# A recurrence with a two-layer network behind it, on one core: the network's blocks go from 384 to 512 tokens, the middle layer is done in halves, and transposes of the later chunks move from TensorE to VectorE

## The chip, the core and the metric

The program runs on one core of a Trainium2 chip. The metric is device microseconds per execution. The kernel before was run three times: 488.08, 490.09 and 491.03 us, a median of 490.09. One more execution was recorded by the hardware profiler; all rows of the profile come from that one.

## The reference: what is computed

The inputs are r, k, v, w of shape batch 4 x heads 8 x sequence 768 x 48, u of heads 8 x 48, and the weights U (768 x 32), V (32 x 768), w1 (384 x 1536) and w2 (1536 x 384).

```
for t in range(S):                                    # a state of 48 x 48 per batch and head
    cur = einsum('bhd,bhe->bhde', u * k[t], v[t])
    y[t] = einsum('bhd,bhde->bhe', r[t], state + cur)
    state = w[t][..., None] * state + einsum('bhd,bhe->bhde', k[t], v[t])
x = y as (batch, 768, 384)                            # heads side by side
h = (x transposed @ U @ V) transposed                 # mixes the 768 tokens of a batch, rank 32
u2 = x + h
out = u2 + maximum(u2 @ w1, 0) @ w2
```

The sequence ahead is serial in the tokens; the mixing needs all tokens of a batch; the network (FFN) behind it needs each token for itself alone.

## The kernel before, in words

**Chunks.** The recurrence is cut into 24 chunks of 128 tokens, six for each batch (`chunk`). For each chunk VectorE runs two scans over the decay w (F, L367, and Q, L380) and scales r and k with them (rk, L387 and L392). TensorE then multiplies scaled k with scaled r to scores for each head (aps, L495), VectorE merges these into a tile A under a mask (L498), A's diagonal comes from r, k and u on other engines (dv, then L430 or L432), and two rounds of matmuls make the chunk's output y: A times v (L555 and L565), and the state of the chunks before times r (L578 and L582). The state is carried on in Z: k is transposed to have tokens on the partitions (four transposes of 128 x 128 in `turn_k`, trk, L482, copied to SBUF as kn by ScalarE), kn times v makes the chunk's addition (dS, L505), and VectorE adds and decays it (Z). The last chunk of a batch hands on no state, so its k isn't transposed. ScalarE copies y to xT (L598), which has channels on the partitions.

**Mixing.** xT of each chunk is transposed (`turn`, three transposes, trx, L616) and copied to xn (L620). For each batch `token_mix` multiplies xn of its six chunks with U (ga, L640), sums up four row groups (gb, L651), and splits the result into a high part and a remainder (gs). `make_u` multiplies it with V (hp, L690) and VectorE adds that to xT (L694).

**FFN.** It is done in 8 blocks of 384 tokens, two for each batch. All its factors are float32 numbers split into a high part and a remainder, and each product is made of three: high x high, remainder of the weight x high, high x remainder. `make_u` splits xT into u (L699 and L705). `ffn` makes 12 *up* steps for a block (f, L738), one for each 128 rows of the middle layer: nine matmuls of 128 x 128 weights against 384 tokens, into one of three PSUM tiles. For each, ScalarE or VectorE takes the maximum with zero as hh (L745 or L747) and VectorE the remainder hl (L751). Then, for each of three output tiles, four *down* steps of nine matmuls (L774) take in 3 of the 12 rows of the middle layer each, all four into the same PSUM tile, VectorE adds it to xT (`total`, L789), and SyncE sends the 128 x 384 piece out (`send`, L793). So there are 192 FFN steps, 1,728 matmuls, and 24 adds at L789. Twelve pairs of hh and hl are held at most.

**Weights.** They arrive as 64-bit numbers and are decoded on the chip, in 24 pieces for w1 and w2 and a few for U and V (`split_raw`): ScalarE, VectorE (L291 to L304) and GpSimd make a float32 number, ScalarE or VectorE the high part, GpSimd or VectorE the remainder (w1l and w2l, L321). This is work of the run's first part.

**Fillers.** `warm` (L180) issues bfloat16 matmuls that compute nothing that is used, into a PSUM tile that the next step overwrites. A step can have some of them ahead of it (`lead`).

**What sets the order.** Every piece of work is a step with its engine. A table of three-character entries, ORDER, gives the sequence in which all steps are issued; `plan` replays it. The first two characters are the step's number, the third says whether the step goes to its other engine and how many fillers stand ahead of it. Each engine executes its own steps in that sequence, and waits at a step until what it needs is there. `plan` also counts the buffers of each kind against `caps` (3 PSUM tiles for the FFN, `ffn`; 12 pairs of the middle layer, `hid`; 1 PSUM tile for transposes, `tr`; and so on).

Of the kernel before, what the change touches and what calls it, by code (L numbers as in the profile page):

```python
# [33 lines left out]
RAW_BUFS, TURNING, CVA_BUFS, KR_BUFS, W_BUFS, RK_BUFS = 7, 4, 3, 2, 2, 4  # L34
# [3 lines left out]
def channel_order():  # L38
# [25 lines left out]
    "06m09R02K09q03206n02509016r0AG01s03312o02L01t08R06p06u06s02O01u09116t01v06q06x02708T02M13D01w08U06v02606y06w"
    "09E02q08V02802Q02903F02R02A06z02B09N02S02f02C01x12D12p06++8r03E02r07108s13G06-"
    "02s02h03H07002T08t07407212U01O03I02V17507303J02g02i03K03402t07602j08u01Q07702k09g08v08W13603L18g07802l01P079"
    "08e09p08h02u03e0A702m03M02v01R08k82n18f02w13507A01S08l03709S11T03808w13f08m03907B03g03h08n09H08i03O03i09J09T"
    "09208j19G03A09409301U03V07C03B09503C01V01W09903N03P07D09M13W03X03Q09I09K07M09A03R0A607N07Q09L19B0AZ09607E07O"
    "09C07R09i03S09W09707S07F09D07T17G0AF09X07P17U09809b07V03Y07W09c09j09U09d03Z09k1D409V09l07X17Y09m09e07Z09Y03a"
    "0AY09f07b07a09n1A809Z03b07e07c09a0Ah03c17d03d17f09o13T19wCA909y09x03j09+0AB03U07g08609-"  # L70
    "03k0AA03l07H0AE1A019r1Ab0AM07h09s1AN0Ag1Ac19t03m0AQ07i1Ai07I09u07j0AH1AC07k08S0AD0D30Ad0AI07J07l07m09v0AJ07n"
    "09z0DD0AK0DC0Aj1AL1AO0Ae07o0A10AP0DT0Af1A20Aa07p0DE0Ao0DU0AR07K0AS1DF07q07L0Dc0Ak1D608707r0Al0DG0Am1Dd07s07t"
    "0E30DW0A30A40DB17u07w0A50DX0D707v0An0D80Db0Ap0Av07x0De0AT07y0D90AU0D50880AV0Dw0E41Dv0DY0DA1AW07z0Df0AX0DH0Dg"
    "0Aq0E51EV07+1DI0E20Ar07-"
    "0DV0Dy0DJ0Dh1EM0800E60As0Dz0E11Ex0DK0DL0EW1810DZ0At0Eo0DN0820Di0Au0EL0D+0DM0830Da1DO1EX1D-"
# [12 lines left out]
    "0IY0Fk0Fo0Iy0Jg1K50Fl0K00JK0Fp0IZ0Jk0JL0Iz0Jh0Fh0JN0J-0Fi0Jl0Fj0JO0K61Jw0I+0Fm1K80JM0I-"
    "0Fn1Fq0K70Jm0Gk0Fr0Fs0K90Go1Gl1Fv0Gs1Gp1Gt1Jn0Fy0Fw0Ft1Jo1Fx0Fu0F-"
    "0Fz1F+0GQ0G01G10G20G50G31G40G80G60G70GR0G91GA0GB0GE0GC0GD0GH0GF0GG0GK0GI0GJ0GN0GL0GM0GS0GO0GP0GT0GW0GU0GV0GX"  # L90
    "0GY0GZ0Gc0Ga0Gb0Gd0Ge0Gf0Gu0Gg0Gh0Gx0Gv1Gw0G+0Gy0JP0Gz0H10G-"
    "0H00JQ0H21H40JR0H30H70H50H60HA0H80H90HS0HB1HC0HT0Jp0Jq0HD0Jr0HG0HE1HF0HJ0HH0HI0HM0HK0HL0HP0HN0HO0HU0HQ1HR0Js"
    "0KA0Jt0KB0KF0KC0HV0KD0HW0HY0KE0HX0KG0HZ0KH0KI0Ha0KJ0KK0KL0KP0Hb0KM0KQ0KN1KR1KT0KO0He0Hc0KU0Hd0KS1KV0LN0KW1LR"
    "0Hf0LO0LS0LP0LT0LQ0Hg0LU1Hh0LV0KX0Hi0LW0Hj0LX1LY1Ka0KY0KZ0Kd0Kb1Kc0Kg0Ke0Kf0L50Kh0Ki0Kj0Km0Kk1Kl0Kp0Kn1Ko0L6"
    "0Kq0Kr0Ks0Kv0Kt1Ku0Ky0Kw0Kx0L70Kz0K+0K-"
    "0L20L00L10L30L40L80LB0L90LA0LC0LD0LE0LH0LF0LG0LI0LJ0LZ0LK0La1Lb0Lc0LL0LM0Lf0Ld0Le0Li0Lg0Lh0M70Lj0Lk0Ll0Lo0Lm"
    "1Ln0Lr0Lp1Lq0M80Ls0Lt0Lu0Lx0Lv1Lw0L+0Ly1Lz0M90L-"
    "0M00M10M40M21M30M51M60MA0MD0MB0MC0ME0MF0MG0MJ0MH0MI0MK0ML0MM0MN0MO0"
# [52 lines left out]
def rwkv_moe_kernel(ctx, tc, wT, rkT, vN, rkN, uB, uT, uD, U, V, w1, w2, out):  # L151
# [9 lines left out]
    hidp = pool("hidp", 24)  # L161
# [20 lines left out]
    def lead(to):  # L182
        if leading[0]:
# [4 lines left out]
    make_identity(nc, ident)  # L188
    maskf = const.tile([P, P], F32, name="maskf")
# [26 lines left out]
    caps = dict(w=W_BUFS, rk=RK_BUFS, kr=KR_BUFS, v=2, F=2, Q=1, A=2, dv=2, kn=2, Z=2, tr=1, aps=1, y=1, dS=1, ffn=3, xT=3, xn=NCH,  # L216
                hid=12, raw=RAW_BUFS, turning=TURNING, cva=CVA_BUFS, g4=1, gs=1, qd=1)

    def step(name, eng, fn, after=(), take=(), use=(), alt=None):

        s = Step(name, eng, fn, after, list(take), list(use), alt)
        steps.append(s)
        return s
# [105 lines left out]
    def chunk(g):  # L329
# [657 lines left out]
```

## Time and profile before

| | us |
|---|---|
| three runs | 488.08, 490.09, 491.03 |
| the profiled execution | 493.23 |
| its span (first to last instruction) | 491.4 |
| TensorE matmuls busy | 467.2 (95%) |
| TensorE weight loads busy | 419.8 (85%) |
| VectorE busy | 315.2 (64%) |
| ScalarE busy | 169.5 (34%) |
| GpSimd busy | 114.6 (23%) |

PE is TensorE's matmuls, PEld its weight loads, which run beside them, DVE is VectorE, ACT ScalarE, POOL GpSimd, SP SyncE; a small q behind one of these names is its queue of issued work. A matmul's recorded duration reaches from its start to its modelled end, and matmuls overlap in the pipeline: the 576 matmuls of the first FFN group are recorded at 344 ns each but take up 158.1 us together. So the time from one matmul to the next is read from starts or from long unbroken stretches, not from a matmul's duration. A group's row gives the line of the program, the engine, the operation, the tile written and the tiles read, the shapes and the number of instructions, then after the bar the busy time in us and the mean duration in ns, and after the second bar the idle time of that engine just ahead of these instructions, with what ended most of it. The chain of waits is the work that ended last, followed back from the last instruction.

### The profile page before, as it was taken

The page shows a single profiled execution, that of the slowest core. Times are in us where ns is not written, and L with a number is a line of the kernel's source. Part 1 is how long each engine was busy: PE and PEld are TensorE (multiplying, and loading weights), DVE is VectorE, ACT ScalarE, POOL GpSimd, SP SyncE. Part 2 cuts the span into 40 slices and gives each one's busy share as a digit, 9 for nine tenths or more (in the row PEclk, how much of TensorE's full clock was granted, in tenths as well). Part 3 has the DMA queues.
Part 4 walks back from the last instruction along what each step waited for, and adds up shares of the span by engine and source line. Part 5 has one row for each costly group of instructions (what it writes and reads, how often), then busy time and mean ns, then how long its engine had stood idle before and what let it go on. Part 6 is the DMA issues. An engine that isn't in the chain of part 4 may idle for free.

```text
span 491.4 us, 9913 instructions
## 1 busy us (share of the span) xinstructions
PE 467.2 (95%) x4116; PEld 419.8 (85%) x4116; DVE 315.2 (64%) x543; ACT 169.5 (34%) x430; POOL 114.6 (23%) x106
## 2 busy tenths in 40 slices
PE   7799889998999999999999999999999999999994
PEld 3577647887889889999988989799999989999994
DVE  8966888999899989961486983683123344412420
ACT  5666665755543453310146430531011221101000
POOL 3513444424454435400061400130000010000000
PEclk9656999999999999999999999999999999999998
DMA  8825864544423583400254630300000000000001
GB/s 295 258 70 173 232 234 128 176 130 147 148 85 88 168 269 111 108 1 16 79 166 120 192 99 33 99 21 0 17 32 1 1 34 17 1 27 23 0 18 37
DMA packets 20644, 47.38 MB, mean 96 GB/s; under 512 B 2480, under 2 KB 8880, under 8 KB 20592
## 3 DMA queue, kind: packets, MB, share of 16 engines
q1 hardware_dynamic: 20592, 46.67, 30.0%
q8 instruction: 34, 0.56, 0.5%
q14 instruction: 18, 0.15, 0.1%
HBM read 41.94 MB, written 4.72 MB: 95 GB/s over the span
## 4 chain that ended last, share of the span: by engine, by line
PE 57%; DVE 21%; DMA 10%; ACT 4%; issue 4%; POOL 2%; SPq 0%; POOLq 0%; DVEq 0%; ACTq 0%
PE f L774 23%; PE f L738 22%; DMA raw_w<-in_w 4%; DMA w<-in_wT 3%; DVE Q L380 3%; DVE F L367 3%; DMA rk<-in_rkT 3%; PE aps L495 2%; DVE cva_w L297 2%; DVE hl L751 2%; PE y L555 1%; PE trk L482 1%; PE y L565 1%; DVE rk L392 1%; PE dS L505 1%
## 5 line engine op out<-in xcount | busy, mean ns | idle before, releaser
L738 PE MATMUL f<-u,w1h 128*128 128x384 f32 x576 | 158.1, 344 | 2.0 <-DVE hl L751 1.4
L738 PEld LDWEIGHTS f<-u,w1h 128*128 128x128 f32 x576 | 105.4, 188 | 4.8 <-DVE hl L751 2.5
L774 PE MATMUL f<-hh,w2h 128*128 128x384 f32 x288 | 100.0, 347 | 0.0
L738 PE MATMUL f<-u,w1l 128*128 128x384 f32 x288 | 97.6, 339 | 0.0
L774 PE MATMUL f<-hh,w2l 128*128 128x384 f32 x288 | 97.5, 339 | 0.0
L751 DVE SCALAR_TENSOR_TENSOR hl<-f,hh 128x384 fp32r<-128x384 f32 x96 | 52.5, 552 | 34.6 <-ACT hh L745 33.4
L745 ACT ACTIVATE hh<-f 128x384 fp32r<-128x384 f32 x56 | 27.3, 488 | 128.0 <-PE f L738 128.0
L774 PE MATMUL f<-hl,w2h 128*128 128x384 f32 x288 | 66.3, 338 | 0.0
L774 PEld LDWEIGHTS f<-hh,w2h 128*128 128x128 f32 x288 | 54.0, 188 | 3.5 <-issue 1.7
L774 PEld LDWEIGHTS f<-hh,w2l 128*128 128x128 f32 x288 | 54.1, 188 | 0.3
L738 PEld LDWEIGHTS f<-u,w1l 128*128 128x128 f32 x288 | 54.1, 188 | 0.2 <-DVE w1l L321 0.2
L774 PEld LDWEIGHTS f<-hl,w2h 128*128 128x128 f32 x288 | 52.0, 188 | 0.0
L789 DVE TENSOR_TENSOR xT<-f,xT 128x384 f32<-128x384 f32 x24 | 13.3, 553 | 55.6 <-PE f L774 55.5
L747 DVE TENSOR_SCALAR hh<-f 128x384 fp32r<-128x384 f32 x40 | 22.2, 554 | 32.2 <-PE f L738 32.0
L304 POOL TENSOR_TENSOR cva_w<-cva_w,raw_w 128x384 int32<-128x384 int32 x24 | 29.8, 1247 | 40.8 <-DVE cva_w L297 21.7
L432 POOL TENSOR_SCALAR_AFFINE_SELECT A<-dv 128x512 f32<-128x512 f32 x23 | 19.5, 855 | 84.4 <-PE y L565 46.4
L498 DVE COPY_PREDICATED A<-maskf,aps 128x1024 f32<-128x1024 uint32 x24 | 31.4, 1307 | 7.1 <-PE aps L495 4.6
L367 DVE TENSOR_TENSOR_SCAN F<-w,resets 128x517 f32<-128x517 f32 x24 | 32.5, 1354 | 2.5 <-DMA w<-in_wT 1.4
L430 ACT ACTIVATE A<-ident,dv 128x128 f32<-128x128 f32 x100 | 31.6, 390 | 5.1 <-DVE dv L461 2.3
L495 PE MATMUL aps<-rk 48*128 48x128 f32 x384 | 30.6, 303 | 2.2 <-DVE rk L392 1.3
L495 PEld LDWEIGHTS aps<-rk 48*128 48x128 f32 x384 | 25.7, 204 | 6.1 <-issue 2.6
L380 DVE TENSOR_TENSOR_SCAN Q<-w,qd 128x516 f32<-128x516 f32 x24 | 30.5, 1273 | 0.0
(117 smaller groups left out, 596.3 us busy)
## 6 DMA issues: line engine op xcount, KB each, us to landing
rk<-in_rkT SPq DMA_DIRECT2D x24, 512.0 KB, 4.6
raw_w<-in_w SPq DMA_DIRECT2D x24, 384.0 KB, 4.2
kr<-in_rkN SPq DMA_DIRECT2D x18, 384.0 KB, 3.7
w<-in_wT SPq DMA_DIRECT2D x24, 258.5 KB, 2.9
v<-in_vN SPq DMA_DIRECT2D x24, 224.0 KB, 3.2
out_dram<-xT SPq DMA_DIRECT2D x24, 192.0 KB, 1.9
raw_V<-in_V SPq DMA_DIRECT2D x6, 96.0 KB, 5.7
raw_U<-in_U SPq DMA_DIRECT2D x1, 192.0 KB, 5.0
```

The source lines that it names most:

```text
L304: lambda: nc.gpsimd.tensor_tensor(out=d["to"].bitcast(I32), in0=d["a"].bitcast(I32), in1=d["e"], op=ALU.add),
L367: nc.vector.tensor_tensor_scan(out=F[:, ::-1], data0=st["w"][:, ::-1], data1=resets[:, ::-1], initial=1.0, op0=ALU.mult, op1=ALU.add)
L380: nc.vector.tensor_tensor_scan(out=st["Q"], data0=st["w"][:, 0:n], data1=qd, initial=0.0, op0=ALU.mult, op1=ALU.add)
L430: nc.scalar.activation(A[:, i, j], ident, AF.Copy, scale=dv[:, NP * i + j : NP * i + j + 1])
L432: nc.gpsimd.affine_select(out=A[:, i], in_=dv[:, NP * i : NP * i + NP].unsqueeze(2).broadcast_to([P, NP, P]), pattern=[[0, NP], [1, P]], c ...
L495: nc.tensor.matmul(aps[:, i, j, :], rk[r, 1, j, :], rk[r, 0, j, :], start=True, stop=True)
L498: nc.vector.copy_predicated(flat(st["A"]), mask8, flat(st["aps"]))
L738: nc.tensor.matmul(ps, wt[:, f, ct, :], u[ct][:, z], start=(n == 0), stop=(n == 8))
L745: nc.scalar.activation(hh, d["ps", f], AF.Relu)
L747: nc.vector.tensor_scalar(out=hh, in0=d["ps", f], scalar1=0.0, scalar2=None, op0=ALU.max)
L751: nc.vector.scalar_tensor_tensor(out=hl, in0=d["ps", f], scalar=0.0, in1=hh.bitcast(F32), op0=ALU.max, op1=ALU.subtract)
L774: nc.tensor.matmul(d["o", ct], wt[:, 4 * ct + part, f - 3 * part, :], hid[f][z], start=(part == 0 and n == 0), stop=(part == 3 and n == 8),)
```

## The change

**Wider blocks.** The 24 chunks are put into 6 FFN blocks of 4 chunks, 512 tokens, over the batches' borders: blocks 1 and 4 hold two chunks each of two batches. Their mixing product and add come in two parts of 256 tokens (`pieces_of`, `make_u`), and their output goes out in two transfers. All tiles of the FFN become 512 wide. The mixing still goes by batch.

**Half the middle layer at a time.** A block does six up steps, then for each output tile two down steps and an add to xT, then the other six up steps, two down steps and another add. Eight pairs of hh and hl are held at most (12 before). The buffers for raw weights, which u uses as well, become 6 (7), each wider; those for xn become 4 (6). There are now 144 FFN steps, 1,296 matmuls of 512 columns, and 36 adds of 512 columns (L871).

**Transposes.** The k of chunks 12 to 23 (ten of them carry a state) and the x of chunks 18 to 23 are transposed by VectorE, straight from SBUF to SBUF: four steps for each chunk, each of four instructions that turn 32 x 32 pieces (`turn_blocks`, L661). These are 160 instructions for k, of 32 partitions x 128 elements, and 96 for x, of 32 x 96. The transposes on TensorE and ScalarE's copies of them go for these chunks.

**Not used.** A way of making a weight's remainder on TensorE is in the code for the pieces in SPLIT_PE, which is empty. One more constant tile (`minus`) is made by one ScalarE instruction.

**A new ORDER.** The table is written anew. It issues 197 fillers instead of 154. Three places of it follow.

TensorE at the start of the first block, as the change has it (f_0_0 and f_0_1 are the PSUM tiles of the first and second up step, trk those of a transposed k; L185 are the fillers):

```order
L185 MATMUL f_0_0_1061<-resets 128x384
L819 MATMUL f_0_0_1061<-u_0_995,w1h 128x512
...
L819 MATMUL f_0_0_1061<-u_2_1056,w1h 128x512
L185 MATMUL trk_1096<-resets 128x384
...
L509 MATMUL trk_1096<-ident,rk_828 128x128 x4
L537 MATMUL dS<-v_998,kn_1116 48x48 x8
...
L185 MATMUL f_0_1_1293<-resets 128x384
L819 MATMUL f_0_1_1293<-u_0_995,w1h 128x512
...
L819 MATMUL f_0_1_1293<-u_2_1056,w1h 128x512
L819 MATMUL f_0_2_1321<-u_0_995,w1h 128x512
```

Between the first and the second up step of the block stand the recurrence of several chunks and fillers; from the second on the up steps follow one another. Before, sixteen FFN steps stood ahead of the scores of chunk 6.

TensorE before, where the k of chunk 14 (rk_2144) is transposed between two up steps:

```order
L738 MATMUL f_1_0_1_2516<-u_0_1_2437,w1h 128x384
L738 MATMUL f_1_0_1_2516<-u_0_2_2453,w1h 128x384
L482 MATMUL trk_2532<-ident,rk_2144 128x128 x4
L738 MATMUL f_1_0_2_2537<-u_0_0_2374,w1h 128x384
L738 MATMUL f_1_0_2_2537<-u_0_0_2374,w1l 128x384
```

and in the change, where that part of the run has only the scores of chunk 13 (rk_1882) between FFN steps:

```order
L819 MATMUL f_1_6_2363<-u_1_2199,w1h 128x512
L819 MATMUL f_1_6_2363<-u_2_2225,w1h 128x512
L527 MATMUL aps_2385<-rk_1882 128x128 x8
L855 MATMUL f_1_0_0_2328<-hh_3_2321,w2h 128x512
L855 MATMUL f_1_0_0_2328<-hh_3_2321,w2l 128x512
```

The transposes of k have left TensorE's row of work here; the FFN steps before and after are wider.

VectorE in the change, where the k of chunks 12 and 13 (rk_1801 and rk_1882) is transposed:

```order
L530 COPY_PREDICATED A_1841<-maskf,aps_1873 128x1024
L661 STREAM_TRANSPOSE kn_1922<-rk_1801 32x4x32 x4
L443 TENSOR_TENSOR kr_1834<-kr_1834,u_rep 128x384
L577 TENSOR_TENSOR Z_1885<-Z_1885,tots 128x384
L440 TENSOR_TENSOR kr_1704<-kr_1704 128x384
L394 SCALAR_TENSOR_TENSOR F_1946<-w_1341,resets 128x517
L661 STREAM_TRANSPOSE kn_1922<-rk_1801 32x4x32 x4
L871 TENSOR_TENSOR xT_392<-f_0_0_2_1629,xT_392 128x512
L443 TENSOR_TENSOR kr_1704<-kr_1704,u_rep 128x384
L430 RECIPROCAL qd<-F_1946 128x4
L661 STREAM_TRANSPOSE kn_2015<-rk_1882 32x4x32 x4
```

The four steps of a chunk's transpose stand apart, with scans, merges and the FFN's adds (L871) between them.

The diff, cut to its core:

```
-RAW_BUFS, TURNING, CVA_BUFS, KR_BUFS, W_BUFS, RK_BUFS = 7, 4, 3, 2, 2, 4
+RAW_BUFS, TURNING, CVA_BUFS, KR_BUFS, W_BUFS, RK_BUFS, XN_BUFS, HID = 6, 4, 3, 2, 2, 4, 4, 8
+BLOCKS = (4, 4, 4, 4, 4, 4)
+TW = 4 * P
+TURN_K_DVE, TURN_X_DVE = range(12, 24), range(18, 24)
 ORDER = (
-    "3n03p01g01F04C00001X03s03r04E03y03u03o03v04D01h01i04e01j01G01k01H05301I01l04L04d04F00200103t13q01Z01J04H01m0"
+    "0003r00G00Y01p03n03q04C03p00100203o00300H00404E00500I00J00604D00a00K00Z00L00701q00b00M01r03y03s02N04L00c01s0"
...
-    hidp = pool("hidp", 24)
+    hidp = pool("hidp", 2 * HID)
...
+        def turn_k_blocks(i):
+            if i == 0:
+                st["kn"] = sb2.tile([P, NP, P], F32, tag="kn", name=f"kn_{g}")
+            turn_blocks(st["kn"], st["rk"][:, 1], i)
...
-            btr = Buf("tr")
-            kt = step("KT " + nm, "PE", turn_k, [ks], take=[btr, buf["kn"]], use=[buf["rk"]])
-            kn = step("KN " + nm, "ACT", copy_k, [kt], use=[buf["kn"], btr])
+            if g in TURN_K_DVE:
+                kn = ks
+                for i in range(4):
+                    kn = step(
+                        "KD " + nm, "DVE", lambda i=i: turn_k_blocks(i), [kn], take=[buf["kn"]] if i == 0 else [],
+                        use=[buf["rk"], buf["kn"]],
+                    )
+            else:
+                btr = Buf("tr")
+                kt = step("KT " + nm, "PE", turn_k, [ks], take=[btr, buf["kn"]], use=[buf["rk"]])
+                kn = step("KN " + nm, "ACT", copy_k, [kt], use=[buf["kn"], btr])
...
+    def turn_blocks(to, src, i):
+        for j in range(4):
+            nc.vector.transpose(
+                to[32 * j : 32 * j + 32, :, 32 * i : 32 * i + 32], src[32 * i : 32 * i + 32, :, 32 * j : 32 * j + 32]
+            )
...
-        for ct in range(NCT):
-            bps = Buf("ffn")
-            for part in range(4):
+        for half in range(2):
+            for f in range(6 * half, 6 * half + 6):
...
+            for ct in range(NCT):
+                bps = Buf("ffn")
+                for part in (2 * half, 2 * half + 1):
...
+                o = sums[ct] = step(
+                    f"O {q}.{half}.{ct}", "DVE", total, [prev, sums.get(ct)] + d["uls"], use=[bps, bx], width=W
                 )
...
+                if half:
+                    step(f"OUT {q}.{ct}", "SP", send, [o], use=[bx], width=W).n = len(d["parts"])
```

More of the change, by code (lines that the diff above doesn't have):

```diff
@@ L99 @@
+    "0Ks1Kt0Kl0Kk0Km0Ko0Kn0Kp0Ku0Kq0Kx0Kv1Kw0K+0Ky1Kz0L10K-"
+    "0L00L40L21L30L70L50L60L80LB0L90LA0LC0LF0LD0LE0LG0LH0LI0"
 )
@@ L602, in chunk, with pieces_of @@
+        bx = xbuf[q]
+        x = step("XE " + nm, "ACT", out_x, [y] + (xs_done[g - 1, "x"] if pos else []), take=[bx] if pos == 0 else [], use=[buf["y"], bx])
+        xs_done[g, "x"] = [x]
         xs_done[b, c] = [x]
-        turn(b, c, [x], bx, buf["xn"])
+        turn(b, c, [x], q, pos, bx, buf["xn"])
+    place_of = [(q, i) for q, n in enumerate(BLOCKS) for i in range(n)]
     blocks, xbuf, xs_done, xns = {}, {}, {}, {}
-    def turn(b, c, after, bx, bxn):
-        blk, cc = divmod(c, TB // P)
-        btr = Buf("tr")
-        d = {}
+    def pieces_of(q):
+        gs = [g for g, (r, _) in enumerate(place_of) if r == q]
+        for b in sorted({g // NCH for g in gs}):
+            mine = [g for g in gs if g // NCH == b]
+            lo = (mine[0] - gs[0]) * P
+            yield b, slice(lo, lo + len(mine) * P), (mine[0] % NCH) * P
@@ new lines, in turn_blocks, with turn, blocks_of_x @@
+    def turn_blocks(to, src, i):
+        for j in range(4):
+            nc.vector.transpose(
+                to[32 * j : 32 * j + 32, :, 32 * i : 32 * i + 32], src[32 * i : 32 * i + 32, :, 32 * j : 32 * j + 32]
+            )
+    def turn(b, c, after, q, cc, bx, bxn):
+        btr = Buf("tr")
+        d = dict(buf=bxn)
+        xns[b, c] = d
+        def blocks_of_x(i):
+            if i == 0:
+                d["xn"] = sb2.tile([P, NCT, P], F32, tag="xn", name=f"xn_{b}_{c}", bufs=XN_BUFS)
+            turn_blocks(d["xn"], blocks[q][:, :, cc * P : (cc + 1) * P], i)
+        if b != "g" and b * NCH + c in TURN_X_DVE:
+            last = after
+            for i in range(4):
+                last = [step(
+                    f"XD {b}.{c}", "DVE", lambda i=i: blocks_of_x(i), last, take=[bxn] if i == 0 else [], use=[bx, bxn],
+                )]
+            d["steps"] = last
+            return
@@ L705, in low @@
                 ENG[eng].tensor_tensor(
-                    out=u[:, 1], in0=blocks[b, blk][:, ct, :], in1=u[:, 0].bitcast(F32), op=ALU.subtract
+                    out=u[:, 1], in0=blocks[q][:, ct, 0:W], in1=u[:, 0].bitcast(F32), op=ALU.subtract
                 )
-            nm = f"{b}.{blk}.{ct}"
-            hp = step(
-                "HP " + nm, "PE", mix, [gs["step"], hp] + ready.get(("V", blk), []), take=[bhp], use=[gs["buf"]],
-            )
-            xs = [s for c in range(3 * blk, 3 * blk + 3) for s in xns[b, c]["steps"] + xs_done.get((b, c), [])]
@@ L714, in make_u @@
-            ad = step("UADD " + nm, "DVE", add, [hp] + xs, use=[bhp, bx])
-            uh = step(
-                "UH " + nm, "ACT", high, [ad] + ups[-1:], take=[bu], use=[bx], alt="DVE"
-            )
+            nm = f"{q}.{ct}"
+            uh = step("UH " + nm, "ACT", high, ads[ct] + ups[-1:], take=[bu], use=[bx], alt="DVE", width=W)
             ups.append(uh)
-            ul = step("UL " + nm, "Pool", low, [uh], use=[bx, bu], alt="DVE")
+            ul = step("UL " + nm, "Pool", low, [uh], use=[bx, bu], alt="DVE", width=W)
@@ L880, in general @@
             for blk in range(2):
-                make_u("g", blk)
-                ffn("g", blk, dst=dst)
+                make_u(("g", blk), [("g", slice(0, TB), blk * TB)])
+                ffn(("g", blk), dst=dst)
+            first = next(s for s in steps if s.name == "GA g.0")
+            steps.remove(first)
+            steps.insert(next(n for n, s in enumerate(steps) if s.name == "XT g.4"), first)
             for s in steps:
@@ L897, in rwkv_moe_kernel @@
         token_mix(b)
-        for blk in range(2):
-            make_u(b, blk)
-            ffn(b, blk)
+        for q in range(len(BLOCKS)):
+            last = max(g for g, (r, _) in enumerate(place_of) if r == q)
+            if last // NCH == b:
+                make_u(q, list(pieces_of(q)))
+                ffn(q)
     with tc.manual_schedule():
```

328 lines of the change are left out of this document (177 added, 151 removed).

## The prediction

> **What bounds the kernel now.** I read the busy times by stage first, then the chain that ended last, then single matmuls on the timeline, then the groups by shape. The stages:
>
> ```profile
> 0.00:72.00 72.00, 59.79 (x659) 42.63 (x660) 57.65 (x94) 46.82 (x128) 28.14 (x30) 0.81 0.66 215
> 72.00:113.00 41.00, 39.01 (x222) 32.36 (x220) 38.95 (x81) 24.25 (x56) 15.39 (x15) 1.00 0.43 136
> 113.00:202.00 89.00, 86.47 (x920) 76.45 (x921) 83.55 (x136) 39.57 (x102) 42.51 (x37) 1.00 0.46 141
> 202.00:324.00 122.00, 120.76 (x1313) 110.72 (x1314) 79.69 (x131) 39.24 (x103) 26.24 (x24) 1.00 0.30 92
> 324.00:485.00 161.00, 161.00 (x1007) 157.63 (x1005) 54.77 (x103) 19.64 (x42) 2.32 (x3) 1.00 0.04 15
> ```
>
> The columns are length, then busy time of matmuls, weight loads, VectorE, ScalarE and GpSimd, then the granted clock. From 113 us on TensorE is busy 86.47 of 89, 120.76 of 122 and 161 of 161 us at clock 1.00: it sets the end. VectorE is second, 38.95 of 41 and 83.55 of 89 us, then ever less. Between 72 and 113 us the first FFN block waits for weights that VectorE splits, and filler matmuls stand in the gaps. The chain agrees, and gives the price of an FFN matmul:
>
> ```profile
> 205.31 0.44 PE trk L482 x4
> ...
> 208.93 0.33 PE trx L616 x3
> 209.25 12.72 PE f L738 x72
> 221.97 11.13 PE f L774 x63
> 233.10 0.49 PE dS L505 x16
> 233.59 1.09 PE aps L495 x16
> ...
> 235.18 0.59 PE trk L482 x4
> ```
>
> Each row is a start, a length and what TensorE did. 12.72 / 72 and 11.13 / 63 are both 0.1767 us from one matmul of 384 columns to the next. What a block of 512 costs depends on why that is not less. The fillers, bf16 with as many columns, go faster, and the edge between an FFN matmul and a transpose tells more:
>
> ```profile
> 71.02 1.62 PE L180 MATMUL f<-resets 128*128 128x384 bf16 x9 [0.30 <-DVE xT L694]
> L180 PE MATMUL f<-resets 128*128 128x384 bf16 x83 | 14.2, 326 | 0.3 <-DVE xT L694 0.3
> ...
> 204.62 0.69 PE L738 MATMUL f<-u,w1h 128*128 128x384 f32 x3
> 204.97 0.53 PEld L482 LDWEIGHTS trk<-ident,rk 128*128 128x128 f32 x4
> 205.15 0.60 PE L482 MATMUL trk<-ident,rk 128*128 128x128 f32 x4
> 205.47 0.19 PEld L738 LDWEIGHTS f<-u,w1h 128*128 128x128 f32 x1
> 205.59 0.19 PEld L738 LDWEIGHTS f<-u,w1l 128*128 128x128 f32 x1
> ...
> L616 PEld LDWEIGHTS trx<-ident,xT 128*128 128x128 f32 x72 | 8.9, 147 | 4.8 <-ACT xT L598 3.2 <-ACT junk L396 0.2 <-ACT raw_w L278 0.2
> ```
>
> Nine fillers take 1.62 us; less the last one's 0.326, eight periods of 0.162 us. The FFN's matmuls are 15 ns slower. It could be their weight load, shown as 0.19 us and back to back. But the third FFN matmul starts at about 204.97, the transpose's load is issued with it, such a load takes 0.15 us, and still the transpose starts only at 205.15, 0.18 later. And behind the short transposes the next FFN load follows its forerunner after 0.12 us (205.47, 205.59), not 0.177. So the 384-column FFN matmul itself holds the array for about 0.177 us, and the load hides behind it.
>
> **The change, part by part.** *Width.* 1,728 matmuls of 384 columns become 1,296 of 512. The trace has no FFN matmul of another width, so the price has two ends. If the 15 ns come per column, 0.1767 x 512/384 = 0.2356 us. If they come per matmul, 128 more columns at the fillers' 0.162/384 add 0.054: 0.2304. No quoted row decides; I take the middle, 0.233. Per token that is only 1% less than now.
>
> The Trainium skill, "TensorE: Matmul & The Clock Gate", section "Back-to-back issue gap", gives N/2.4 + 2.5 ns for a warm matmul, 162.5 at 384 columns and 215.8 at 512. The fillers' 162 agrees with it, the FFN's 177 does not. By it the 1,287 matmuls counted below would take 277.7 us.
>
> *Front.* The new order starts one up step, waits, and from the second up step on carries no fillers but the 18 ahead of the second block. What must be done by then is VectorE's, so I price its steps by their groups' mean durations: 103.7 us of them stand ahead of the scores of chunk 6 in the order before, which began at 113.52, and 101.1 us ahead of the second up step now. At one busy microsecond per microsecond, as in 72 to 113 us, that step starts at 111.
>
> ```profile
> 113.52 0.49 PE L495 MATMUL aps<-rk 48*128 48x128 f32 x4 [1.28 <-DVE rk L392]
> 484.51 0.69 PE L774 MATMUL f<-hl,w2h 128*128 128x384 f32 x3
> 485.83 0.33 SPq L793 DMA_DIRECT2D out_dram<-xT  x1
> ```
>
> *TensorE from there.* Before, 113.52 to 484.51 + 0.69 = 485.2 is 371.7 us. All FFN steps but 16 lie in it: 1,584 x 0.1767 = 279.9. The other 91.8 are the recurrence, the mixing and waits. Now 143 FFN steps of 9 are left: 1,287 x 0.233 = 299.9, so 20.0 more, because only one step instead of 16 is done by then. The other work shrinks, since more chunks are done and transposes have left TensorE: 15 groups of four transposes of k less (0.44 and 0.59 in the chain; 0.45 taken: 6.8), 7 of x (0.33 there; 0.30 taken: 2.1), 2 score groups (1.09: 2.2), 3 state updates (0.49: 1.5), one inner product (its twelve matmuls estimated at 0.9), 3 mixing products more (estimated 0.5): 13.0. That leaves 78.8, with waits as they are. The moves alone give 10 x 0.45 + 6 x 0.30 = 6.3 of it.
>
> *VectorE.* The moved transposes become 160 of 32 x 128 elements and 96 of 32 x 96. The trace has none; the nearest copies:
>
> ```profile
> L205 DVE COPY sel<-sel 128x96 f32<-128x96 f32 x1 | 0.3, 252 | 0.0
> L461 DVE COPY dv<-trd 128x8 f32<-128x8 f32 x2 | 0.3, 159 | 0.8 <-PE trd L454 0.8
> L694 DVE TENSOR_TENSOR xT<-hp,xT 128x384 f32<-128x384 f32 x24 | 12.5, 546 | 1.3 <-PE hp L690 1.3
> L751 DVE SCALAR_TENSOR_TENSOR hl<-f,hh 128x384 fp32r<-128x384 f32 x96 | 52.5, 552 | 34.6 <-ACT hh L745 33.4
> L789 DVE TENSOR_TENSOR xT<-f,xT 128x384 f32<-128x384 f32 x24 | 13.3, 553 | 55.6 <-PE f L774 55.5
> ...
> sum 485.00, PE 467.02 PEld 419.80 DVE 314.61 ACT 169.53 POOL 114.60; mean PE 467.02 PEld 419.80 DVE 314.61 ACT 169.53 POOL 114.60
> ...
> span 491.4 us, 9913 instructions
> ```
>
> 93 ns for 88 elements make 0.252 at 96 and 0.286 at 128 alone. In a row each starts before the last ends: 24 adds of L694 are 12.5 us busy, not 13.1, and three in a row save 0.07 apiece. I take 0.18 and 0.21, together 51 us; the ends are the elements alone (0.10 and 0.14: 32) and no overlap (70). The second add of each output makes 36 wide ones of about 0.69 (0.553 and 128 elements more) out of 24: 11.5 more. The remainders L751 lose 3. So VectorE's 314.6 busy us become about 374. It comes where TensorE covers it: by the order 217 us of mean durations, 206 busy (314.6 busy are 330.8 by means), stand between the second up step and the scores of the last chunk, where TensorE has 222. That is 93%, as in 113 to 202 us, so I charge nothing. Without that cover each microsecond over 222 goes to the end. In VectorE's queue the remainders and adds that free the FFN's three PSUM buffers stand behind the transposes, and TensorE's next step behind those.
>
> *Nothing on the path.* ScalarE loses 16 copies and was at 39.57 of 89. GpSimd's wider subtractions fit 42.51 of 89. The output moves the same bytes. The 43 more fillers (7 us) stand in waits for VectorE, counted in the 111. Fewer buffers for the middle layer (8 for 12) go with only six halves held at once. The last add is 0.1 wider, and 0.1 goes to its transfer.
>
> *Sum.* 111 + 299.9 + 78.8 + (491.4 - 485.2) + 0.2 = 496.1 against a span of 491.4: 4.7 more. The profiled execution took 493.23, the runs' median is 490.09, so 494.8 for the median: 495.
>
> **Rivals.** *The load was the bound after all (B).* For it: loads are 157.63 of 161 busy, and 0.19 is longer than 0.177. The Trainium skill, "Perfetto Trace Analysis", section "Identifying the Most-Contended Engine", would judge TensorE by that share. Against it: the starts at 205.15 and 205.59. Then 512 columns stream at the fillers' rate, 0.162 x 4/3 = 0.216: 1,287 x 0.017 = 21.9 less. TensorE then has only 210 in the stretch where VectorE has 206, and I give 5 back to waits: 478.
>
> *The order pays (C).* The other 91.8 us hold about 13 of waits, since its steps priced singly make 79. If the new order takes two thirds of these, and VectorE's idle 14 us before 72 us are halved so that the second up step starts at 104, 16 less: 479. For it: a table written for several courses of events. Against: the front has as much VectorE work ahead as before, and the middle of the run more.
>
> *VectorE becomes the bound (D), slower.* Place: chunk 12 on, where each transpose of k stands in four pieces between scans and adds. If they overlap nothing (70 us), VectorE has about 223 of TensorE's 222 there, and the state update waits for the last piece. TensorE then loses what it does where VectorE has 94%, 2.5 of 89, and as much again for the late state updates, 12 in all over 222: 507. It decides from about 0.28 us a transpose on.
>
> **How the numbers follow.** A measurement here tells about 1% (5 us) from no change. My case (A) has 0.48: 495, own range 487 to 502, half of it within 1%, nearly the rest slower. B has 0.20, 0.18 of it faster and 0.02 within. C has 0.12, 0.10 faster and 0.02 within. D has 0.20, 0.18 slower and 0.02 within. Of A's 0.48, 0.02 is faster, 0.24 within, 0.22 slower. So faster by over 1%: 0.02 + 0.18 + 0.10 = 0.30; within: 0.24 + 0.02 + 0.02 + 0.02 = 0.30; slower: 0.22 + 0.18 = 0.40. B and C reach down to 472, D up to 511; the range is 471 to 510.
>
> **What would show it.** In the profile after: the 512-column matmuls about 0.233 apart (0.216 speaks for B); the second up step of the first block at about 111 us (104 for C); transposes at 0.2 to 0.29 us each and VectorE at or under 93% of the stretch up to the last chunk's scores (over 97%, with TensorE waiting for remainders or copies, for D); no transposes of k on TensorE from chunk 12 on. The prediction is wrong in its main step if the width alone saves more than 10 us.

## The result and the profile after

The changed kernel is slower: 506.27 us (median of 5 runs, 505.06 to 509.71) against 490.59 before (488.08 to 493.71), a ratio of 1.0339 with a 95% interval of 1.0298 to 1.0379. The forecast was 495. Its profiled execution took 509.71 us with a span of 508.0; before it was 493.23 and 491.4.

The stages of the changed kernel (length, then busy time of matmuls, weight loads, VectorE, ScalarE and GpSimd, then the granted clock):

```profile
0.00:72.00 72.00, 55.30 (x636) 41.24 (x636) 53.27 (x91) 41.75 (x118) 31.06 (x32) 0.79 0.60 197
72.00:113.00 41.00, 33.17 (x273) 20.33 (x270) 38.10 (x71) 22.31 (x53) 13.82 (x10) 1.00 0.39 122
113.00:202.00 89.00, 80.72 (x732) 61.02 (x731) 80.87 (x148) 37.77 (x92) 48.28 (x46) 0.98 0.49 153
202.00:324.00 122.00, 119.47 (x996) 93.76 (x995) 115.36 (x244) 35.50 (x94) 26.09 (x24) 1.00 0.28 87
324.00:485.00 161.00, 160.79 (x959) 126.71 (x958) 91.44 (x198) 22.23 (x49) 9.13 (x8) 1.00 0.05 18
485.00:508.00 23.00, 16.87 (x73) 13.24 (x71) 4.84 (x7) 1.19 (x2) 0.00 (x0) 0.94 0.11 38
```

TensorE is busy 4.5 us less up to 72 us and 5.8 less from 72 to 113 than before, and 5.75 less from 113 to 202, where it had been busy 86.47 of 89. VectorE is at 115.36 of 122 from 202 to 324, where it had 79.69. Behind 324 us nothing is amiss.

The second up step, and the end, on the timeline of TensorE:

```profile
113.26 0.50 PE L819 MATMUL f<-u,w1h 128*128 128x512 f32 x1
115.31 0.50 PE L819 MATMUL f<-u,w1l 128*128 128x512 f32 x1 [1.56 <-POOL w1l L330]
115.65 0.39 PE L819 MATMUL f<-u,w1h 128*128 128x512 f32 x1
...
501.01 0.86 PE L855 MATMUL f<-hl,w2h 128*128 128x512 f32 x3
```

The step starts at 113.26 and stops after its first matmul: the remainder of its weights has only just come from GpSimd. Ahead of it, from the end of the first up step at 91.7 us on, TensorE mostly ran fillers (89 of them, 15.1 us). In its sequence the step stands behind the scores of chunk 7 and the transposed k of chunks 8 to 10, and these wait for VectorE's rk and ScalarE's kn:

```profile
96.84 5.21 PE L185 MATMUL aps<-resets 128*128 128x384 bf16 x31
102.22 1.16 PE L527 MATMUL aps<-rk 48*128 48x128 f32 x16 [0.17 <-DVE rk L414]
...
104.93 5.20 PE L185 MATMUL trk<-resets 128*128 128x384 bf16 x31 [0.96 <-ACT kn L518]
110.49 0.66 PE L509 MATMUL trk<-ident,rk 128*128 128x128 f32 x4 [0.36 <-DVE rk L419]
```

The price of a wide matmul, from the chain that ended last:

```profile
468.27 10.50 PE f L855 x45
478.77 10.50 PE f L819 x45
```

10.50 / 45 is 0.2333 us. VectorE's new groups:

```profile
L661 DVE STREAM_TRANSPOSE kn<-rk 32x128 f32<-32x128 f32 x160 | 48.3, 302 | 2.4
L661 DVE STREAM_TRANSPOSE xn<-xT 32x96 f32<-32x96 f32 x96 | 25.9, 269 | 1.4
L871 DVE TENSOR_TENSOR xT<-f,xT 128x512 f32<-128x512 f32 x36 | 24.7, 687 | 39.0 <-PE f L855 38.8
```

160 x 0.302 is 48.3: nothing overlaps, and the transposes take 74.2 us.

To see where the time went, each stage's time without useful TensorE work is worth more than its busy time: the length less the union of all matmuls but the fillers. Before it is 51.1 us over the span, now 75.0, 23.9 more, while the useful work shrank by 7.3. Of the 23.9, 6.4 lie in the first 40 us, -2.7 from 40 to 72, 12.0 from 72 to 113, and 8.2 behind. The trace has 185 fillers, 31 more than before and not 43: of those that the table counts, 12 stand at steps that issue none.

From the start of TensorE's last stretch on (before: the scores of chunk 6; now: the second up step) the matmuls of each kind, from their start to the next one's, less idle time and fillers, sum up to this (in brackets the number of FFN steps):

| term, us | forecast | before | after | measured |
|---|---|---|---|---|
| start of the stretch | -2.5 | 113.52 | 113.26 | -0.3 |
| FFN steps | +20.0 | 286.7 (176) | 308.1 (143) | +21.4 |
| other TensorE work | -13.0 | 79.8 | 66.6 | -13.2 |
| waits and fillers | 0 | 5.2 | 13.9 | +8.7 |
| from the last matmul to the end | +0.2 | 6.2 | 6.1 | -0.1 |
| sum | +4.7 | 491.4 | 508.0 | +16.6 |

Matmuls overlap and their ends are modelled, so the border between two kinds is not sharp: counted from end to end, the FFN steps are +22.7, the other work -14.9 and the waits and fillers +9.1.

### The profile page after: what moved, and what is told of

It reads as the page before. It is cut to its first block, busy times and chain, and to the rows that moved or that the text cites. A ratio compares the mean times of both kernels' runs of the same rounds, so it can differ in the third digit from the quotient of the medians.

```text
span 508.0 us, 9195 instructions
## 1 busy us (share of the span) xinstructions
PE 466.3 (92%) x3657; PEld 356.3 (70%) x3657; DVE 383.9 (76%) x754; ACT 160.8 (32%) x406; POOL 128.4 (25%) x118
## 4 chain that ended last, share of the span: by engine, by line
PE 53%; DVE 27%; DMA 7%; issue 4%; POOL 4%; ACT 3%; SPq 0%; POOLq 0%; DVEq 0%; ACTq 0%
PE f L855 21%; PE f L819 20%; DMA raw_w<-in_w 5%; DVE kn L661 4%; DVE Q L407 3%; DVE F L394 3%; PE aps L527 3%; DVE hl L832 2%; POOL cva_w L312 2%; PE y L595 2%; DVE A L530 2%; DVE cva_w L305 2%; DMA rk<-in_rkT 1%; PE y L605 1%; DVE xn L661 1%
## 5 line engine op out<-in xcount | busy, mean ns | idle before, releaser
L819 PE MATMUL f<-u,w1h 128*128 128x512 f32 x432 | 143.8, 402 | 6.4 <-DVE hl L832 5.3
L819 PEld LDWEIGHTS f<-u,w1h 128*128 128x128 f32 x432 | 81.3, 188 | 30.0 <-DVE hl L832 7.2
L855 PE MATMUL f<-hh,w2h 128*128 128x512 f32 x216 | 87.3, 404 | 0.6 <-DVE hl L832 0.6
L819 PE MATMUL f<-u,w1l 128*128 128x512 f32 x216 | 85.6, 396 | 1.6 <-POOL w1l L330 1.6
L855 PE MATMUL f<-hh,w2l 128*128 128x512 f32 x216 | 85.4, 395 | 0.0
L832 DVE SCALAR_TENSOR_TENSOR hl<-f,hh 128x512 fp32r<-128x512 f32 x72 | 49.1, 687 | 23.3 <-ACT hh L826 22.1
L826 ACT ACTIVATE hh<-f 128x512 fp32r<-128x512 f32 x39 | 23.2, 595 | 136.7 <-PE f L819 136.5
L855 PE MATMUL f<-hl,w2h 128*128 128x512 f32 x216 | 62.0, 395 | 0.0
L871 DVE TENSOR_TENSOR xT<-f,xT 128x512 f32<-128x512 f32 x36 | 24.7, 687 | 39.0 <-PE f L855 38.8
L661 DVE STREAM_TRANSPOSE kn<-rk 32x128 f32<-32x128 f32 x160 | 48.3, 302 | 2.4
L855 PEld LDWEIGHTS f<-hh,w2h 128*128 128x128 f32 x216 | 40.5, 188 | 11.9 <-issue 1.5
L185 PEld LDWEIGHTS <-resets 128*128 128x128 bf16 x185 | 18.5, 103 | 20.1 <-issue 7.8
```

The costliest lines, as they stand in the source:

```text
L661: nc.vector.transpose(to[32 * j : 32 * j + 32, :, 32 * i : 32 * i + 32], src[32 * i : 32 * i + 32, :, 32 * j : 32 * j + 32])
L819: nc.tensor.matmul(ps, wt[:, f, ct, :], u[ct][:, z], start=(n == 0), stop=(n == 8))
L826: nc.scalar.activation(hh, d["ps", f], AF.Relu)
L832: nc.vector.scalar_tensor_tensor(out=hl, in0=d["ps", f], scalar=0.0, in1=hh.bitcast(F32), op0=ALU.max, op1=ALU.subtract)
L855: nc.tensor.matmul(d["o", ct], wt[:, 4 * ct + part, f - 3 * part, :], hid[f][z], start=(part % 2 == 0 and n == 0), stop=(part % 2 == 1 and ...
L871: nc.vector.tensor_tensor(out=o, in0=d["o", ct], in1=o, op=ALU.add)
```

## The experiments

Two theories: **the transposes** (rival D: VectorE's 74 us more of work make TensorE wait), and **the table** (the new order leaves TensorE without work in the front; the design itself is sound). The tables of x2, x3 and x5 to x11 come from a planner of ours that shifts steps, or gives them to their other engine, by the durations in the traces; each keeps its kernel's steps and buffers. So a table here means the order, the choice between two engines (x5 and x9 change it for some 170 of 1,363 steps each) and the places of the fillers. Ratios are to the kernel before, run on the same chip.

| run | blocks, late transposes, table | us | ratio, 95% interval |
|---|---|---|---|
| change | 512, VectorE, its own | 506.3 | 1.034 (1.030 to 1.038) |
| x1 | 512, TensorE, the change's | 510.0 | 1.039 (1.029 to 1.050) |
| x2 | 512, VectorE, first | 502.2 | 1.026 (1.016 to 1.036) |
| x3 | 384, TensorE, first | 505.6 | 1.031 (1.021 to 1.040) |
| x5 | 512, VectorE, second | 490.1 | 0.999 (0.995 to 1.002) |
| x6 | 384, TensorE, second | 490.8 | 1.000 (0.997 to 1.003) |
| x7 | 384, VectorE, second | 483.6 | 0.987 (0.982 to 0.992) |
| x8 | 512, TensorE, second | 490.1 | 1.000 (0.996 to 1.003) |
| x9 | 512, VectorE, third | 487.2 | 0.992 (0.990 to 0.994) |
| x10 | 384, VectorE, third | 484.0 | 0.987 (0.983 to 0.991) |
| x11 | 384, TensorE, third | 491.9 | 1.004 (1.001 to 1.007) |
| x12 | before, FFN steps late | 528.4 | 1.074 (1.067 to 1.081) |

**x1: the transposes back on TensorE.**

```
-TURN_K_DVE, TURN_X_DVE = range(12, 24), range(18, 24)
+TURN_K_DVE, TURN_X_DVE = (), ()
```

In the table a transpose and its copy stand where the first of VectorE's four steps stood.

> The changed kernel with all its transposes back on TensorE (four for k, three for x, and ScalarE's copy), each at the place in the order where VectorE's first piece of it stood; all else as changed. VectorE loses 256 instructions that start 0.315 and 0.283 us apart there, about 77 us; TensorE gets 10 x 0.48 + 6 x 0.35 = 6.9 us more work. If VectorE's transposes are what made the change slow (rival D), TensorE's waits behind 172 us, where the first of them is issued, go as well, some 5 to 9 us, and the time is at or under 505. If they are hidden (the cost sits in the order of the work: the FFN starts late), TensorE has 6.9 us more and about the waits it had: 511 to 515.

Measured 509.99 (508.46 to 511.44). The same three stages as above:

```profile
72.00:113.00 41.00, 33.67 (x271) 20.35 (x269) 38.48 (x69) 22.50 (x54) 14.83 (x11) 1.00 0.39 123
113.00:202.00 89.00, 83.22 (x752) 63.49 (x753) 71.13 (x119) 38.71 (x93) 50.52 (x49) 1.00 0.49 156
202.00:324.00 122.00, 120.35 (x1018) 95.48 (x1017) 79.40 (x116) 38.92 (x102) 23.07 (x21) 1.00 0.29 85
```

VectorE falls from 115.36 to 79.40 of 122 us, and the time doesn't fall. TensorE's work in the stretch rises by 4.8 us, its waits and fillers fall from 13.9 to 11.9. The time lies between the two cases of the expectation, nearer the second. So the transposes cost about 2 us of waits and spare 5 of work; D's mechanism is not what made the change slow, though D's 507 is nearly the time.

**x2 and x3: a first new table for the changed kernel, and one for the kernel before.**

```
 ORDER = (
-    "0003r00G00Y01p03n03q04C03p00100203o00300H00404E00500I00J00604D00a00K00Z00L00701q00b00M01r03y03s02N04L00c01s0"
+    "3o03z13n03p04C01p01r00Y00703s03u03v01q03w14F03++0Z04H04D03x14L01s01t01u00803y04M04I00b05300a03-11v04400904G1"
...
```

> The changed kernel with another order table, and nothing else changed: the same 1,363 steps, the same widths, halves, buffers and VectorE transposes; a few steps may change to their other engine, as the table allows. In it the FFN steps of the first block start as early as their weights allow. If the order is the cause, the time falls far under 490: TensorE's busy time less fillers is 466 - 197 x 0.163 = 434 us, and with 25 to 45 us of idling around it 460 to 480. If VectorE's 384 busy us and its transposes are the cause, they are all still there, and the time stays above 495.

> The kernel before with another order table and nothing else changed (blocks of 384, all transposes on TensorE). Its TensorE is busy 467 - 154 x 0.163 = 442 us without fillers, 8 more than in the changed kernel. If the order decides, this too falls, to 465 to 485, and the changed design with such an order is 4 to 12 us faster than this one. If the kernel before was bound by its TensorE work in any order, it stays at 485 to 492.

Measured 502.22 and 505.55. By its expectation x2 speaks for the transposes; x5 and x9 below take that back. x3 fits neither case: a new table loses 15 us with the kernel before, too. Both gave GpSimd much more of the front's work. What that did to VectorE, in the groups of the kernel before and of x3 (scan F, the merge, scan Q, one step of the weights; each 24 instructions):

```profile
L367 DVE TENSOR_TENSOR_SCAN F<-w,resets 128x517 f32<-128x517 f32 x24 | 32.5, 1354 | 2.5 <-DMA w<-in_wT 1.4 <-POOL rk L392 1.1
L498 DVE COPY_PREDICATED A<-maskf,aps 128x1024 f32<-128x1024 uint32 x24 | 31.4, 1307 | 7.1 <-PE aps L495 4.6 <-ACT A L430 2.0 <-POOL A L432 0.5
L380 DVE TENSOR_TENSOR_SCAN Q<-w,qd 128x516 f32<-128x516 f32 x24 | 30.5, 1273 | 0.0
L290 DVE TENSOR_SCALAR cva_w<-cva_w 128x384 uint32<-128x384 uint32 x24 | 9.6, 411 | 0.0
```

```profile
L360 DVE TENSOR_TENSOR_SCAN F<-w,resets 128x517 f32<-128x517 f32 x24 | 38.0, 1582 | 1.0 <-DMA w<-in_wT 1.0
L373 DVE TENSOR_TENSOR_SCAN Q<-w,qd 128x516 f32<-128x516 f32 x24 | 35.5, 1479 | 0.4
L491 DVE COPY_PREDICATED A<-maskf,aps 128x1024 f32<-128x1024 uint32 x24 | 31.4, 1308 | 2.0 <-PE aps L488 2.0
L283 DVE TENSOR_SCALAR cva_w<-cva_w 128x384 uint32<-128x384 uint32 x24 | 17.0, 710 | 0.3
```

The instructions that read SBUF alone take 16 to 73% longer; the merge, which reads PSUM, takes the same. So handing VectorE's work to GpSimd is paid for in VectorE's own time. That this is what made x2 and x3 slow isn't shown: x9 and x10 below give GpSimd as much (170 and 156 us, x2 and x3 176 and 158) and are faster than the kernel before.

**x4: widths.**

```
-                    for n, (wt, ct, z) in enumerate(parts):
-                        nc.tensor.matmul(ps, wt[:, f, ct, :], u[ct][:, z], start=(n == 0), stop=(n == 8))
+                    cut = (128, 192, 256, 64, 160, 512)[f % 6]
+                    for cs in (slice(0, min(cut, W)), slice(min(cut, W), W)):
+                        if cs.stop > cs.start:
+                            for n, (wt, ct, z) in enumerate(parts):
+                                nc.tensor.matmul(ps[:, cs], wt[:, f, ct, :], u[ct][:, z, cs], start=(n == 0), stop=(n == 8))
```

> The changed kernel, with each up step's nine matmuls of 512 columns done as nine of the first n columns and nine of the rest, n = 128, 192, 256, 64, 160 and 512 by turns; nothing is left out. The distance from one matmul to the next is read for each width. If the price is per column (0.1767 at 384 and 0.2333 at 512 lie on 0.0069 + 0.000442 a column), 320 columns take 0.148, 256 take 0.120, 192 take 0.092 and 128 take 0.064, unless a floor shows. If the weight load bounds narrow ones, they stop falling at 0.107 (a load of 128 columns behind a short matmul came 0.12 after its forerunner) or, by the recorded 0.188 of a load, already at 320.

Measured 526.33, a single run. Starts on its timeline (its up matmuls are at L822):

```profile
411.51 0.34 PE L822 MATMUL f<-u,w1l 128*128 128x384 f32 x1
411.69 0.34 PE L822 MATMUL f<-u,w1h 128*128 128x384 f32 x1
...
414.16 0.31 PE L822 MATMUL f<-u,w1h 128*128 128x320 f32 x1
414.31 0.31 PE L822 MATMUL f<-u,w1l 128*128 128x320 f32 x1
...
417.31 0.28 PE L822 MATMUL f<-u,w1l 128*128 128x64 f32 x1
417.42 0.28 PE L822 MATMUL f<-u,w1h 128*128 128x64 f32 x1
417.53 0.28 PE L822 MATMUL f<-u,w1l 128*128 128x64 f32 x1
...
418.88 0.37 PE L822 MATMUL f<-u,w1h 128*128 128x448 f32 x1
419.09 0.37 PE L822 MATMUL f<-u,w1l 128*128 128x448 f32 x1
```

Over the run the median distances are 112 ns at 64, 128, 160 and 192 columns, 119 at 256, 147 at 320, 162 at 352, 177 at 384, 205 at 448 and 232 at 512. From 256 on they lie within 2 ns on 0.445 a column and 5 fixed. Below there is a floor of 112; that it is the weight load is argued only, as a matmul of 64 columns has little else. (The second of nine matmuls follows the first sooner, after 30 ns at 64 and 90 at 192 columns; the floor holds from there on.) Either way the price at 384 and 512 is per column, far over the floor, and rival B is out.

**x5 to x8: second tables, for both widths and both places of the transposes.** The planner now knew that VectorE slows beside GpSimd. For x7 the kernel before got the change's `turn_blocks`, `turn_k_blocks` and the two ranges; for x8 the ranges are empty, as in x1. In x5's table one of the 36 adds at L871 stands behind the second half's matmuls of its output tile, so that half is added twice and the first not at all; the work is the same. As its output lacks that half, x9 below, which leaves nothing out, has to bear the argument.

```
 ORDER = (
-    "0003r00G00Y01p03n03q04C03p00100203o00300H00404E00500I00J00604D00a00K00Z00L00701q00b00M01r03y03s02N04L00c01s0"
+    "3n03s00G04d00003u03o03y03p01p00H00203v00J00104C00K04g00L04D04m01r03z14e03w03t14L03x15300300I00M03++4F04H04I0"
...
```

> The changed kernel with a second new order table and nothing else changed. In x2 and x3 GpSimd was given more work (176 and 158 busy us, against 128 and 115), and VectorE's instructions on SBUF operands took longer while it worked (a weight's first steps 0.73 and 0.69 us for 0.44 and 0.41). This table gives GpSimd no more than the changed kernel's, and starts the second up step near 90 us and not at 113. If the place of the first block's FFN steps is what decides, it takes 470 to 488. If the changed design is bound by its VectorE work in any order, it stays over 500, as x2 did.

> The kernel before with a second new order table, GpSimd about as busy as before, chunks 0 to 6 done sooner (scores of chunk 6 near 61 us and not 113) and the first block's FFN steps spread from 65 us on. If its own table leaves something, 470 to 486; if it doesn't, 488 or more. Next to x5 it prices the design with both tables made in one way: TensorE's work alone says that the changed design is 8 to 13 us faster (442 busy us against 434 without fillers).

> The kernel before (blocks of 384) with one part of the change alone: the late transposes of k (chunks 12 to 23) and of x (chunks 18 to 23) on VectorE, and a table made for it in the way of x6's. If VectorE's transposes cost what rival D says, it is slower than x6 by 5 to 15 us; if they lie in VectorE's idle time, it is faster than x6 by the 7 us that TensorE is spared.

> The changed kernel's wide blocks and halves with all transposes on TensorE, and a table made for it in the way of x5's. Against x6 it prices the wide blocks alone: per token TensorE's FFN work is 2% less (311 against 305 us), so 6 us faster if the order can use it, slower if the later start of a 512-token block costs more. Against x5 it prices the transposes alone: 7 us slower than x5 if VectorE hides them.

Measured 490.09, 490.75, 483.55 and 490.12. x5 lies between its two cases, 16 us under the change by its table alone. The kernel before gains nothing from its new one (x6). The VectorE transposes alone (x7 against x6) gain 7.2 us, as much as the work that TensorE is spared. The wide blocks alone (x8 against x6) gain 0.6, under what can be told, where 6 were expected, and both together (x5 against x6) 0.7. Beside wide blocks the VectorE transposes gain nothing (x5 against x8, where 7 were expected): x5's TensorE has 9.9 us less useful work over the span and 11.1 us more without any.

**x9 to x11: third tables.**

```
 ORDER = (
-    "0003r00G00Y01p03n03q04C03p00100203o00300H00404E00500I00J00604D00a00K00Z00L00701q00b00M01r03y03s02N04L00c01s0"
+    "3n03s03o00003y03t14C03u00G03v04F00102N00H00300I00400503p04L00J03z01p03x04G10K01r04d00203++4D00L01q00M02P03r0"
...
```

> The changed kernel with a third order table and nothing else changed; the scores of chunk 6 stand near 57 us, the first two FFN steps of its first block at about 73 and 80, and its further ones follow from 91 on without a gap of 25 us as in the changed kernel (88 and 113). My theory: the change's 16 us lie in the front of its table (18 of its 24 extra us without useful TensorE work come before 113 us), not in its design. Then this takes 468 to 480. The rival (VectorE, with 73 us of transposes more than before, is the bound of this design): x5's 490 or above, as VectorE's work is the same.

> The kernel before with the late transposes on VectorE (blocks of 384), as x7, with a third table. If x7's 483.5 is near what this design can do, 480 to 485; if its table still idled TensorE in the front (33 of 50 us without useful work before 113 us), 468 to 480. Against x9 it prices wide blocks where the transposes are on VectorE: theory 2% less FFN work per token, 3 to 6 us for x9; VectorE bound: x9 slower by 5 or more, as x5 was against x7.

> The kernel before with a third table and nothing else changed, made in the way of x9's and x10's. Against x10 it prices the transposes alone: the theory says 7 to 10 us slower than x10, by the TensorE work that VectorE takes over; if VectorE were the bound, faster than x10.

Measured 487.16, 484.02 and 491.88. x9 is 19 us under the change, with the same steps and buffers. Its stages:

```profile
0.00:72.00 72.00, 59.20 (x675) 43.81 (x676) 66.60 (x87) 49.33 (x145) 48.73 (x41) 0.83 0.64 215
72.00:113.00 41.00, 37.80 (x371) 26.36 (x370) 34.80 (x51) 26.64 (x73) 27.47 (x22) 0.96 0.42 140
113.00:202.00 89.00, 88.85 (x749) 66.36 (x746) 80.01 (x149) 47.81 (x126) 50.23 (x44) 1.00 0.41 132
202.00:324.00 122.00, 122.00 (x1013) 93.67 (x1012) 109.57 (x239) 33.41 (x91) 36.79 (x36) 1.00 0.29 95
```

VectorE is nearly as full as in the change from 113 to 324 us (189.6 against 196.2 busy of 211), and TensorE stands idle for 0.15 us there, not 10.8. Part of that is hidden by fillers: without useful work TensorE is there for 7.6 us, against 13.6 in the change and 5.4 before. Most of the gain lies ahead: up to 113 us TensorE is without useful work for 41.6 us, not 55.0, and has begun 55 FFN matmuls, not 9. Over the span the time without useful work is 55.4 us, not 75.0. It still missed 468 to 480: its first two FFN steps came at 87 and 89 us and not at 73 and 80, and its 55.4 us are more than the 49.8 of x7 and 47.4 of x10. x10 stays at x7's time, its first case. x11 is 7.9 slower than x10, so the transposes on VectorE pay 7 to 8 us with blocks of 384 in two pairs of tables; x9 is 3.1 slower than x10, so the wide blocks don't pay there either. That lies between the two cases of x10's expectation (x9 faster by 3 to 6, or slower by 5 or more). With x5, 6.5 slower than x7, it leaves open that wide blocks and VectorE's transposes together cost TensorE some waits in any of these tables.

**x12: the kernel before with its early FFN steps late.** Its table has the 15 steps, the fillers that stand ahead of them and their hh and hl behind the scores of chunk 6.

```
order of the steps, kernel before       x12
UP 0.0.0                                UP 0.0.0
UP 0.0.1                                AM 6
UP 0.0.2                                UP 0.0.1
...                                     UP 0.0.2
DN 0.0.0.3                              ...
AM 6                                    DN 0.0.0.3
```

(UP and DN are up and down steps, AM 6 the scores of chunk 6.)

> The kernel before with one thing changed in its table: the 15 FFN steps of the first block that stood ahead of the scores of chunk 6, all but its first one, stand right behind them, as far back as the changed kernel has them; nothing else is moved. If what TensorE doesn't do in the front is paid at the end, it is slower by up to 15 x 1.63 = 24.5 us (510 to 520), less what VectorE and TensorE win by being free of these steps there. If the front has room that is otherwise lost, and later waits take the steps in, it is under 500.

Measured 528.39, beyond the upper end. From 72 to 113 us:

```profile
72.00:113.00 41.00, 5.01 (x28) 3.58 (x29) 34.36 (x67) 21.40 (x48) 16.76 (x14) 0.58 0.43 136
113.00:202.00 89.00, 87.66 (x771) 75.81 (x769) 57.12 (x96) 30.70 (x78) 23.55 (x21) 0.98 0.26 80
```

TensorE loses 23.3 us of useful work in the first of the two stages, about the 24.5 of the steps, and 10.3 more in the second up to 172 us. The second loss is fillers. 74 of them, which had stood between 72 and 113 us, came along with their steps, and now stand where the weights of these steps have been there since 99 us:

```profile
112.10 5.86 PE L173 MATMUL f<-resets 128*128 128x384 bf16 x24
...
119.38 3.26 PE L173 MATMUL f<-resets 128*128 128x384 bf16 x19
...
135.20 5.21 PE L173 MATMUL f<-resets 128*128 128x384 bf16 x31
```

At 0.163 apiece they are 12.1 us; with the 24.5 that is 36.6 of the 37.6 us by which x12 is slower. The granted clock was 0.58 in the stage in which TensorE idled. So what isn't done in the front is paid in full, one for one, and fillers that no longer fill a wait are paid for as well.

## Why the prediction was wrong

**The failed step** is "waits as they are" in the sum's term "TensorE from there". The waits and fillers of the stretch were 5.2 us before, not the about 13 that rival C put down, and became 13.9: 8.7 of the 11.9 us by which the sum fell short. The start of the stretch makes 2.3 (113.26 for 111) and the FFN steps 1.4. The 13.0 for the other work was nearly right, 13.2 by the same count: the transposes fell by 9.3 (8.9 reckoned), the state updates by 1.5 (1.5), the products for y by 0.8 (0.9), the score groups by 1.1 and not 2.2, and the mixing products became 3 fewer, not 3 more.

**Where the waits come from.** What TensorE waited for between 113 and 330 us in the changed kernel, the largest rows (us in total, times, longest):

```profile
PE f L819 <- DVE hl L832: 5.3, 3, 1.8
PE f L819 <- POOL w1l L330: 1.6, 1, 1.6
PE gb L721 <- ACT g L716: 1.0, 1, 1.0
```

and in x1:

```profile
PE f L812 <- DVE hl L825: 1.8, 1, 1.8
PE f L812 <- POOL w1l L323: 1.6, 1, 1.6
```

Two of the three waits for hl go with the transposes, 3.5 us; the other two rows stay or come back under another name, and 18 fillers near 197 us, 2.9 us, stand ahead of a transpose of x and of the step that waits for u. In the front the table puts the recurrence ahead of the weights: by 113 us 12 of the 24 pieces of weights were split in two, against 17 before, while VectorE had begun 11 scans F against 8 and done 1.4 us of FFN work against 8.5. So the up steps come late and then meet weights that are late themselves. The number of pieces alone doesn't decide: x9 has 12 pieces and 11 scans by then too, but its FFN steps stand earlier in TensorE's sequence, six of them from 87 us on and ahead of 113. x1 takes 73 us of work from VectorE, and 2.0 us of waits and fillers go; x9 keeps that work, and its TensorE has 19.6 us less without useful work, 13.4 of them ahead of 113 us. That the table is the cause is shown by x9, with the same steps and buffers and 19 us less; which of its many differences weighs how much isn't, as x5 and x9 move hundreds of steps at once. The smaller numbers of buffers (8 pairs for 12, 6 raw for 7) aren't the cause: x9 has them too.

**Front: right in the number, wrong in its bearing.** 111 was forecast and 113.26 measured. But the prediction compared only VectorE's work ahead of two different events and took what TensorE left undone as given (20.0 us more FFN work behind). That was the largest term, 21.4 as measured, and it is the table's doing, not the width's: with blocks of 512 as well, x9 has begun 55 FFN matmuls by 113 us and x8 56, the change 9.

**Width: right.** 0.233 forecast, 0.2333 measured, per column by x4. A step took 2.15 us with its hand-overs (308.1 / 143), against 1.63 (286.7 / 176). Per token that is 1% less, as the prediction had it, and not the 2% of the expectations of x8 and x10.

**The Trainium skill's N/2.4 + 2.5 ns** ("TensorE: Matmul & The Clock Gate", section "Back-to-back issue gap") gives 215.8 ns at 512 columns; the page calls it the gap of an isolated matmul and gives about 131 ns at 512 for a stream. x4's 232 in a stream agrees with neither, nor did the 177 at 384 with the rule; the sum by that rule, 22 us lower, was rightly not taken.

**VectorE: sized wrong, with little consequence here.** The transposes took 0.302 and 0.269 us each, over the upper ends of 0.286 and 0.252, and 74 us in all, not 51. VectorE had 93% of the stretch up to the last scores, as forecast (227.76 of 243.99 us). By rival D's own point, 0.28 us, it should have decided; by x1 it cost 3.5 us of waits for hl, not the 12 that D put down, and 5 us of TensorE's work were spared.

**Rivals.** B falls by x4, C by the result, D as the cause of this loss by x1 and x9. The case that happened, a table that idles TensorE more than the one before, was not among them: C had its opposite only.

## What to carry to other kernels

Where an order is a table, judge a change to it by what the bound engine leaves undone at a fixed moment in each kernel, in us of its work; that debt is paid at the end, in x12 one for one. Leave fillers out of the count, and move a step without the fillers that stood ahead of it. Compare two designs only with orders made in the same way: the late transposes on VectorE alone are worth 7 us with blocks of 384 (483.6 against 490.8, faster than both kernels), and the 512-token blocks nothing that shows, alone or with them. A time that agrees with a rival's number is no evidence for its mechanism.

## What the runs showed of the hardware

GpSimd's work slows VectorE's, by operands. In the traces of both kernels and of x1 to x3, scan F took 1.224 us where no GpSimd instruction ran (65 instructions) and 1.683 where one ran all the time (22); the first two steps of a weight 0.349 and 0.850 (122 and 48). The merge took 1.307 and 1.306, the remainders hl, the adds and the transposes of 32 x 128 (0.302 both) showed no difference. The Trainium skill says so in "SBUF — State Buffer", section "Who interferes with whom": an instruction with two SBUF inputs, and copies, casts and tensor_scalar in a two-port mode, share a port pair with GpSimd. The traces agree for these groups.

An instruction of 32 x 32 block transposes on VectorE takes 33 ns for 32 elements more (0.302 against 0.269 at 128 and 96), which leaves about 170 fixed (an estimate from these two), and unlike the adds of three in a row before (24 of 0.546 in 12.5 us) these instructions don't overlap. In x4's streams, with a weight load of 128 columns for each, TensorE's matmuls of split float32 numbers came about 112 ns apart at 64 to 192 columns, from the third of nine on.
